# Exchanging heads in the loads of the last six pairs instead of in GpSimd's casts

## The chip, the cores and the metric

The kernel runs on one core of a Trainium2 chip. The metric is the device time of one execution in microseconds (us). The kernel before takes 314.71 us (median of 3 runs, 314.62 to 314.78). Profiles are of one execution each; their "span" goes from the first to the last instruction of the program, and the device time holds a little more around it.

The core has five engines that run side by side, each with its own queue of instructions in a fixed order: TensorE (PE; its weight loads are PEld), VectorE (DVE), ScalarE (ACT), GpSimd (POOL) and SyncE (SP), which in this kernel issues DMAs. They wait for each other through semaphores.

## The reference

A retention layer (attention with a decay in place of a softmax) and a bilinear feed-forward layer on its output.

```python
# q, k, v: [8 batches, 8 heads, 576 tokens, 64]
scores = scale * np.matmul(q, k.transpose(0, 1, 3, 2))
gamma = 1.0 - 2.0 ** (-5.0 - np.arange(H))
rel = pos[:, None] - pos[None, :]
Dmat = np.where(rel >= 0, gamma[:, None, None] ** rel, 0.0)
attn_out = np.matmul(scores * Dmat, v)
x = attn_out.transpose(0, 2, 1, 3).reshape(4608, 512)
a, b = x @ w_a, x @ w_b            # 512 -> 1536
out = (a * b) @ w_out              # 1536 -> 512
```

Inputs and the output are float32; the kernel multiplies in bfloat16.

## The kernel before

**Tiling.** The 4608 tokens are taken in 18 pairs of 256 tokens. For the first three the code works in steps of its own; from then on every pair n has two blocks of 128 tokens (kp = 0, 1), one token per partition, so that a pair's q, k or v is a tile of 128 partitions by 1024 float32: 2 blocks x 8 heads x 64. Pairs 15 and 17 (`LEFT`) gather the last 64 tokens of four batches each. The feed-forward layer works on blocks of 512 tokens (two pairs), with 12 slices of its hidden width. The last five blocks use combined sums of weights, rows and products (Strassen-like) to save matmuls.

**Why heads change places.** TensorE multiplies 64x64 pieces, four at a time, in the four quarters of its array. So the two heads of a head pair c and the two halves (64 tokens) of a block are matched crosswise: in partitions 64 to 127 of `qkb`, the bfloat16 tile that holds q and k of a pair, the two heads of each head pair stand in exchanged places (`keyed`, L662: `64 * (r ^ a)`). Before the change, GpSimd makes this exchange while it converts.

**A pair's way.** The function names and lines are those of the listing:
- `load_pair(n)` (L163): SyncE loads q, k and v from HBM into float32 tiles `qf`, `kf`, `vf` (L171), one DMA per block; for pairs 15 and 17 one per batch (four of 64 partitions). The tiles are in turn, two of each kind.
- `ahead(n)` (L564): GpSimd makes `qkb` and `vb`. For n >= `MIXED` (6) q is multiplied by a decay per token and head from the table `qs2` (`decayed_queries`: L579 for partitions 0 to 63, L584 for partitions 64 to 127, with the heads exchanged); k is converted (L605, and L609 with the exchange); v is multiplied by its decay from `vs2` (L616).
- `turn(n)` (L625): SyncE issues two DMA transposes, q and k of `qkb` into `qkT` (L633). For n > 10 it then calls `load_pair(n + 2)`.
- `stretch(n, n - 1)` (L847): TensorE opens the outputs of pair n - 1 from the states (L763), multiplies keys and values of pair n (`keyed`, L664), its scores (`matched`, L735, the first use of the pair's `qkT`) and closes the outputs of pair n - 1 (L776).

**Order.** The program is written out by hand: TensorE's matmuls are counted, and the list `todo` says at which count each of these functions is called. Each engine then runs its instructions in the order of these calls. On SyncE, load 12, the transposes of pair 11, load 13, the stores of a block's output (`store_mixed`, L997) and the transposes of pair 12 stand behind each other, and so on. On GpSimd the work of `ahead` shares the queue with sums of the output (L1071) and gated products (L1239). SyncE's DMAs count on eight semaphores in turn, so that a DMA also waits until the one eight places before it has landed.

**Tables.** `pair_tables` (L267) fills `vs2` and `qs2` in the opening phase: VectorE makes an index, and ScalarE takes exponentials of it, one for each head (L276, L278). `lgp` (L228) holds the logarithms of the decays, of even heads in partitions 0 to 63 and of odd heads in partitions 64 to 127.

Of the kernel before, what the change touches and what calls it, by code (L numbers as in the profile page):

```python
# [10 lines left out]
FP32 = mybir.dt.float32  # L11
BF16 = mybir.dt.bfloat16
INT32 = mybir.dt.int32
AF = mybir.ActivationFunctionType
# [4 lines left out]
def kernel(  # L19
# [10 lines left out]
    nc = tc.nc  # L30

    B, H, S, D = q.shape
    DM = H * D
# [4 lines left out]
    HP = H // 2  # L38
    scale = 1.0 / math.sqrt(D)
    gammas = [1.0 - 2.0 ** (-5.0 - h) for h in range(H)]  # L40
# [5 lines left out]
    LEFT = {NP - 3: 0, NP - 1: 1}  # L46
# [5 lines left out]
    PAIRS = [(0, 0), (1, 0), (2, 0), (0, 1), (1, 1), (2, 1)]  # L52
# [6 lines left out]
    def part_of(n):  # L59
        return PAIRS[n][1]  # L60
# [4 lines left out]
    def rows_of(n):  # L65

        if n not in LEFT:
            b, m = PAIRS[n]
            return [(kp, 0, 128, b, 256 * m + 128 * kp) for kp in (0, 1)]
        return [(i // 2, 64 * (i % 2), 64, 4 * LEFT[n] + i, S - 64)  # L70
                for i in range(4)]

    def pool(name, bufs, space=None):
        kw = {} if space is None else {"space": space}
        return ctx.enter_context(tc.tile_pool(name=name, bufs=bufs, **kw))

    const = pool("const", 1)
# [67 lines left out]
    def half(i):  # L145
        return slice(64 * i, 64 * i + 64)
# [10 lines left out]
    def staged(n, name, its_name):  # L157

        extra = n < MIXED + 3 and n % 3 == 2
        return (begin if extra else stage).tile(  # L160
            [128, 2 * DM], FP32, tag=name, name=its_name)

    def load_pair(n, which=(0, 1, 2)):  # L163
        if n >= NP:
            return
        paired.setdefault(n, {})
        for i in which:
            name, src = (("qf", q), ("kf", k), ("vf", v))[i]
            t = staged(n, name, name + "2")
            for kp, r0, m, b, s0 in rows_of(n):  # L170
                nc.sync.dma_start(  # L171
                    t[r0:r0 + m, kp * DM:(kp + 1) * DM]
                    .rearrange("p (h d) -> p h d", h=H),
                    src[b, :, s0:s0 + m, :].rearrange("h s d -> s h d"))
            paired[n][i] = t

    def load_step(n, hh, which, on=nc.sync):
# [11 lines left out]
    Q, K, V = 0, 1, 2  # L189
# [36 lines left out]
    idxp_f = const.tile([128, 2], FP32)  # L226
    nc.vector.tensor_copy(idxp_f, idxp_i)
    lgp = const.tile([128, HP], FP32)  # L228
    for c in range(HP):
        nc.vector.memset(lgp[0:64, c:c + 1], math.log(gammas[2 * c]))  # L230
        nc.vector.memset(lgp[64:128, c:c + 1], math.log(gammas[2 * c + 1]))
    biasq = const.tile([128, 1], FP32)
    nc.vector.memset(biasq, math.log(scale))
    vs = const.tile([128, H, 2], FP32)
    for h in range(H):
        nc.scalar.activation(vs[:, h, :], idxp_f, AF.Exp,
                             bias=0.0, scale=-math.log(gammas[h]))
# [10 lines left out]
    idxv = const.tile([128, 3, 2], FP32)  # L248
    vs2 = const.tile([128, 3, 2, H], FP32)

    qs2 = const.tile([128, 3, 2, H], FP32)
# [14 lines left out]

    def pair_tables(step):  # L267
        if step == 0:
            nc.vector.tensor_copy(idxv, idxv_i)
            nc.vector.tensor_scalar_add(idxv[:, 2, 1:2], idxv[:, 2, 1:2],  # L270
                                        -128.0)
            nc.vector.tensor_scalar_add(idxv[64:128, 2], idxv[64:128, 2],
                                        -64.0)
        else:
            for h in (2 * step - 2, 2 * step - 1):
                nc.scalar.activation(vs2[:, :, :, h], idxv, AF.Exp,  # L276
                                     bias=0.0, scale=-math.log(gammas[h]))
                nc.scalar.activation(qs2[:, :, :, h], idxv, AF.Exp,  # L278
                                     bias=biasq[:, 0:1],
                                     scale=math.log(gammas[h]))  # L280

    state_after = begin.tile([128, 2, HP, 128], BF16)
    own_sums = [begin.tile([128, HP, 64], FP32, name=f"own{n}")
# [280 lines left out]
    def ahead(n):  # L564


        qkb = nat.tile([128, 2, 2 * DM], BF16, tag="qkb", name="qkb2")
        vb = nat.tile([128, 2 * DM], BF16, tag="vb", name="vb2")
        halves = [slice(0, DM), slice(DM, 2 * DM)]
        whole = [slice(0, 2 * DM)]  # L570
        part = 2 if n in LEFT else part_of(n)

        def per_head(t):
            return t.rearrange("p (h d) -> p h d", d=D)

        def decayed_queries(t):
            by = qs2[:, part].rearrange("p k h -> p (k h)")
            for hs in (slice(0, H), slice(H, 2 * H)):
                nc.gpsimd.tensor_tensor(  # L579
                    per_head(qkb[0:64, Q])[:, hs], per_head(t[0:64])[:, hs],  # L580
                    by[0:64, hs].unsqueeze(2).to_broadcast([64, H, D]),
                    op=ALU.mult)
            for r in (0, 1):
                nc.gpsimd.tensor_tensor(  # L584
                    per_head(qkb[64:128, Q])[:, 1 - r::2],
                    per_head(t[64:128])[:, r::2],
                    by[64:128, r::2].unsqueeze(2).to_broadcast([64, H, D]),
                    op=ALU.mult)

        if n >= MIXED:  # L590
            decayed_queries(paired[n].pop(Q))
        if n >= BY_ACT:
            t = paired[n].pop(K)
            to, fro = (x.rearrange("p (j r d) -> p j r d", r=2, d=D)
                       for x in (qkb[64:128, K], t[64:128]))
            key_casts[n] = [
                lambda: nc.scalar.copy(qkb[0:64, K], t[0:64])] + [
                lambda r=r: nc.scalar.copy(to[:, :, 1 - r], fro[:, :, r])
                for r in (0, 1)]
            copies_due.extend([lambda: key_casts[n].pop(0)() if key_casts[n]  # L600
                               else None] * 3)
        for w in () if n >= BY_ACT else (K,) if n >= MIXED else (Q, K):
            t = paired[n].pop(w)
            for e in halves:
                nc.gpsimd.tensor_copy(qkb[0:64, w, e], t[0:64, e])  # L605
                to, fro = (x.rearrange("p (j r d) -> p j r d", r=2, d=D)
                           for x in (qkb[64:128, w, e], t[64:128, e]))
                for r in (0, 1):
                    nc.gpsimd.tensor_copy(to[:, :, 1 - r], fro[:, :, r])  # L609
        t = paired[n].pop(V)  # L610
        decay = (vs2[:, part].unsqueeze(3)
                 .to_broadcast([128, 2, H, D])
                 .rearrange("p k h d -> p (k h) d"))
        for e in halves:
            at = slice(e.start // D, e.stop // D)
            nc.gpsimd.tensor_tensor(  # L616
                vb[:, e].rearrange("p (h d) -> p h d", d=D),
                t[:, e].rearrange("p (h d) -> p h d", d=D),
                decay[:, at], op=ALU.mult)
        natural[FIRST + n, "pair"] = (qkb, vb)  # L620
# [4 lines left out]
    def turn(n):  # L625
        while key_casts.get(n):
            key_casts[n].pop(0)()
        qkb = of(natural, n)[0]
        qkT = qkt_pool.tile([128, 2, 2, HP, 128], BF16, tag="qkT",
                            name="qkT2")  # L630
        transposed[FIRST + n, "pair"] = qkT
        for w in (Q, K):
            nc.sync.dma_start_transpose(  # L633
                qkT[:, w].rearrange("p k c s -> p (k c) s"), qkb[:, w])
        if n > 10:
            load_pair(n + 2)
# [913 lines left out]
    for i, which in ((4, Q), (4, K), (4, V), (5, Q), (5, K), (5, V)):  # L1550
        load_step(*STEPS[i], which)
    load_pair(FIRST)
    load_pair(FIRST + 1, (Q,))


# [94 lines left out]
    for fn, places in ((ahead, casts), (turn, turns)):  # L1650
        todo += [(at, fn, (n,)) for n, at in places.items()]
# [46 lines left out]
```

## Time and profile before

| what | us |
|---|---|
| device time, median of 3 runs | 314.71 |
| device time of the profiled execution | 314.71 |
| its span | 313.0 |
| TensorE busy | 303.0 |
| GpSimd busy | 202.8 |
| VectorE busy | 224.0 |
| ScalarE busy | 156.0 |

The profile's page has the busy time of each engine, the chain of work that ended last (followed back from the last instruction), and groups of instructions by line and shape with their mean duration and the idle time of the engine before them. Its map of the span in 40 slices has these two rows, busy tenths of TensorE and of GpSimd:

```profile
PE   7899999999999999999999999999999999999994
...
POOL 3990079665996649867799769985999350035413
```

A slice is 7.8 us. TensorE is over 90% busy in all but the first two and the last. GpSimd is close to full in many slices between 40 and 245 us. The clock that TensorE was granted is 0.998 of full speed over the span.

### The profile page before, as it was taken

The page shows a single profiled execution, that of the slowest core. Times are in us where ns is not written, and L with a number is a line of the kernel's source. Part 1 is how long each engine was busy: PE and PEld are TensorE (multiplying, and loading weights), DVE is VectorE, ACT ScalarE, POOL GpSimd, SP SyncE. Part 2 cuts the span into 40 slices and gives each one's busy share as a digit, 9 for nine tenths or more (in the row PEclk, how much of TensorE's full clock was granted, in tenths as well). Part 3 has the DMA queues.
Part 4 walks back from the last instruction along what each step waited for, and adds up shares of the span by engine and source line. Part 5 has one row for each costly group of instructions (what it writes and reads, how often), then busy time and mean ns, then how long its engine had stood idle before and what let it go on. Part 6 is the DMA issues. An engine that isn't in the chain of part 4 may idle for free.

```text
span 313.0 us, 9645 instructions
## 1 busy us (share of the span) xinstructions
PE 303.0 (97%) x3922; PEld 198.6 (63%) x3955; DVE 224.0 (72%) x450; ACT 156.0 (50%) x351; POOL 202.8 (65%) x290
## 2 busy tenths in 40 slices
PE   7899999999999999999999999999999999999994
PEld 3554457868544554557874787468746875687774
DVE  5745337758757765768878886888679968877873
ACT  7755346626433554455455545544635554335530
POOL 3990079665996649867799769985999350035413
PEclk9999999999999999999999999999999999999999
DMA  8999999999999999999999989948703020013004
GB/s 213 256 202 207 247 240 198 197 216 182 208 171 231 174 204 191 218 244 285 190 260 228 179 180 227 192 83 182 213 10 70 24 112 2 2 53 85 1 2 134
DMA packets 144797, 50.97 MB, mean 163 GB/s; under 512 B 126576, under 2 KB 141680, under 8 KB 144752
## 3 DMA queue, kind: packets, MB, share of 16 engines
q1 hardware_dynamic: 138272, 45.10, 70.9%
q0 software_dynamic: 5808, 4.72, 9.6%
q8 instruction: 31, 0.51, 0.7%
q10 hardware_dynamic: 672, 0.52, 0.5%
q14 instruction: 14, 0.11, 0.1%
HBM read 37.75 MB, written 9.44 MB: 151 GB/s over the span
## 4 chain that ended last, share of the span: by engine, by line
PE 91%; DVE 2%; DMA 2%; SPq 2%; issue 2%; ACT 1%; DVEq 0%; ACTq 0%
PE m L1047 16%; PE pb L1419 13%; PE pa L1398 12%; PE pb L1284 9%; PE pa L1284 9%; PE po L1445 8%; PE lm L1227 7%; PE ls L1227 3%; DMA qf<-in_q_dram 2%; SPq L182 2%; PE la L1227 2%; PE po L933 2%; PE sc L735 2%; PE o L763 1%; PE kv L664 1%
## 5 line engine op out<-in xcount | busy, mean ns | idle before, releaser
L1424 DVE TENSOR_TENSOR hT<-ha,pb 128x512 bf16<-128x512 bf16 (+1 forms) x60 | 34.6, 579 | 32.4 <-PE pb L1419 28.4
L1419 PE MATMUL pb<-xT,wb_sb 128*128 128x512 bf16 (+1 forms) x237 | 49.9, 336 | 0.3
L1398 PE MATMUL pa<-xT,wa_sb 128*128 128x512 bf16 (+1 forms) x238 | 47.6, 326 | 0.5 <-issue 0.3
L1412 ACT CAST ha<-pa 128x512 bf16<-128x512 f32 (+1 forms) x60 | 29.8, 500 | 34.3 <-PE pa L1398 31.8
L1071 POOL TENSOR_TENSOR osb<-crossed,straight 128x256 f32<-128x256 f32 x24 | 17.5, 756 | 44.3 <-ACT crossed L1059 44.3
L1419 PEld LDWEIGHTS <-wb_sb 128*128 128x128 bf16 x240 | 23.4, 98 | 17.8 <-issue 0.5
L1398 PEld LDWEIGHTS <-wa_sb 128*128 128x128 bf16 x244 | 23.3, 98 | 16.5 <-DVE sums L691 0.2
L579 POOL TENSOR_TENSOR qkb<-qf,qs 64x512 bf16<-64x512 f32 x24 | 24.7, 1044 | 13.1 <-DMA qf<-in_q_dram 8.2
L1284 PE MATMUL pb<-xT,wb_sb 128*128 128x512 bf16 x125 | 32.1, 379 | 0.2
L616 POOL TENSOR_TENSOR vb<-vf,vs 128x512 bf16<-128x512 f32 x30 | 30.8, 1046 | 2.0 <-DMA vf<-in_v_dram 0.8
L1284 PE MATMUL pa<-xT,wa_sb 128*128 128x512 bf16 x119 | 31.4, 379 | 0.7 <-issue 0.3
L1047 PEld LDWEIGHTS <-hT 128*128 128x128 bf16 x288 | 28.1, 98 | 5.0 <-DVE hT L981 0.5
L1294 ACT CAST ha<-pa 128x512 bf16<-128x512 f32 x32 | 18.7, 585 | 24.6 <-PE pa L1284 24.6
L1297 DVE TENSOR_TENSOR hT<-ha,pb 128x512 bf16<-128x512 bf16 x32 | 21.9, 684 | 10.0 <-PE pb L1284 8.1
L609 POOL CAST qkb<-kf 64x256 bf16<-64x256 f32 x60 | 27.7, 488 | 1.5
L1445 PE MATMUL po<-wo_sb,hT 128*128 128x512 bf16 x113 | 26.7, 379 | 0.8 <-issue 0.6
L584 POOL TENSOR_TENSOR qkb<-qf,qs 64x512 bf16<-64x512 f32 x24 | 26.7, 1134 | 0.7
L1047 PE MATMUL m<-wo_sums,hsum 128*128 128x256 bf16 x216 | 25.7, 273 | 0.0
L981 DVE TENSOR_TENSOR hsum<-hT 128x512 bf16<-128x512 bf16 (+2 forms) x51 | 23.5, 493 | 0.5
L605 POOL CAST qkb<-kf 64x512 bf16<-64x512 f32 x30 | 20.3, 677 | 5.4 <-DMA kf<-in_k_dram 4.0
L1047 PEld LDWEIGHTS <-hsum 128*128 128x128 bf16 x216 | 21.1, 98 | 2.4
L1284 PEld LDWEIGHTS <-wb_sb 128*128 128x128 bf16 x128 | 12.3, 98 | 14.3
(159 smaller groups left out, 578.4 us busy)
## 6 DMA issues: line engine op xcount, KB each, us to landing
qf<-in_q_dram SPq DMA_DIRECT2D x32, 256.0 KB, 5.4
vf<-in_v_dram SPq DMA_DIRECT2D x32, 256.0 KB, 5.0
kf<-in_k_dram SPq DMA_DIRECT2D x31, 256.0 KB, 5.1
out_dram<-osb SPq DMA_DIRECT2D x9, 512.0 KB, 4.2
out_dram<-osb SPq DMA_DIRECT2D x22, 128.0 KB, 2.8
wo_sb<-in_moe_w_out_dram POOLq DMA_DIRECT2D x3, 512.0 KB, 15.9
out_dram<-osb SPq DMA_DIRECT2D x6, 256.0 KB, 4.1
qf<-in_q_dram SPq DMA_DIRECT2D x8, 128.0 KB, 3.3
```

The costliest lines, as they stand in the source:

```text
L579: nc.gpsimd.tensor_tensor(per_head(qkb[0:64, Q])[:, hs], per_head(t[0:64])[:, hs], by[0:64, hs].unsqueeze(2).to_broadcast([64, H, D]), op= ...
L584: nc.gpsimd.tensor_tensor(per_head(qkb[64:128, Q])[:, 1 - r::2], per_head(t[64:128])[:, r::2], by[64:128, r::2].unsqueeze(2).to_broadcast( ...
L609: nc.gpsimd.tensor_copy(to[:, :, 1 - r], fro[:, :, r])
L616: nc.gpsimd.tensor_tensor(vb[:, e].rearrange("p (h d) -> p h d", d=D), t[:, e].rearrange("p (h d) -> p h d", d=D), decay[:, at], op=ALU.mult)
L1047: nc.tensor.matmul(to, rows, cols, start=(begins and p == 0), stop=True, skip_group_check=True)
L1227: nc.tensor.matmul(to[:, m], w[:, c], x[:, c], start=(way in (1, 2, 5) and m == c == 0), stop=True, skip_group_check=True)
L1284: nc.tensor.matmul(p1, w[:, c, F * 128:F * 128 + 128], xT[:, c], start=(c == 0), stop=(c == NC - 1))
L1398: nc.tensor.matmul(pa[:, at:at + width], wa_sb[:, c, fs], xT[:, c, at:at + width], start=(c == at == 0), stop=(c == NC - 1), skip_group_ch ...
L1412: nc.scalar.copy(ha[:, 0:n], pa[:, 0:n])
L1419: nc.tensor.matmul(pb[:, 0:n], wb_sb[:, c, fs], xT[:, c], start=(c == 0), stop=(c == NC - 1))
L1424: nc.vector.tensor_tensor(hT[:, F, 0:n], has[F][:, 0:n], pb[:, 0:n], op=ALU.mult)
L1445: nc.tensor.matmul(po, hT[:, F, u * 128:(u + 1) * 128], wo_sb[:, F], start=(F == 0), stop=(F == NF - 1))
```

## The change

For pairs 12 to 17 (`PLACED = 12`) the loads of q and k already put the heads of tokens 64 to 127 of each block in exchanged places. A new function `places_of` gives, for each of the two blocks, three DMAs in place of one: partitions 0 to 63 with all eight heads, the even heads of partitions 64 to 127 into the odd places, and the odd heads into the even places. (For pairs 15 and 17 six take the place of four.) v is loaded as before. With the heads in place, GpSimd decays q with two products over 128 partitions in place of four over 64, and converts k with two casts over 128 partitions in place of two of 64x512 and four of 64x256.

The decay table `qs2` now holds, in partitions 64 to 127, the decay of the exchanged head; its exponentials take their factor from `lgp` or from a new table `lgq` (eight memsets on VectorE in `pair_tables`) in place of a constant. Pairs 6 to 11, which still exchange heads in GpSimd, read the table at `1 - r` instead of `r`.

```diff
+    PLACED = 12
+
+    def places_of(n, t, src):
+
+        heads = t.rearrange("p (k j r d) -> p k j r d", k=2, r=2, d=D)
+        if n in LEFT:
+            b0 = 4 * LEFT[n]
+            lower, upper = (src[b0 + a:b0 + 4:2, :, S - 64:S, :].rearrange(
+                "k (j r) s d -> s k j r d", r=2) for a in (0, 1))
+        else:
+            b, m = PAIRS[n]
+            lower, upper = (src[b, :, 256 * m:256 * m + 256, :].rearrange(
+                "(j r) (k a s) d -> a s k j r d", a=2, k=2, r=2)[a]
+                for a in (0, 1))
+        k = (0, 1)
+        return [(to[:, ks], fro[:, ks]) for ks in k for to, fro in (
+            (heads[0:64].rearrange("p k j r d -> p k (j r) d"),
+             lower.rearrange("s k j r d -> s k (j r) d")),
+            (heads[64:128, :, :, 1], upper[:, :, :, 0]),
+            (heads[64:128, :, :, 0], upper[:, :, :, 1]))]
...
-            for kp, r0, m, b, s0 in rows_of(n):
-                nc.sync.dma_start(
...
+            if i == V or n < PLACED:
+                for kp, r0, m, b, s0 in rows_of(n):
+                    nc.sync.dma_start(
...
+            else:
+                for to, fro in places_of(n, t, src):
+                    nc.sync.dma_start(to, fro)
...
+    lgq = const.tile([128, HP], FP32)
...
+            for c in range(HP):
+                for i in (0, 1):
+                    nc.vector.memset(lgq[half(i), c:c + 1],
+                                     math.log(gammas[2 * c + 1 - i]))
...
-                                     bias=biasq[:, 0:1],
-                                     scale=math.log(gammas[h]))
+                nc.scalar.activation(
+                    qs2[:, :, :, h], idxv, AF.Exp, bias=biasq[:, 0:1],
+                    scale=(lgq if h % 2 else lgp)[:, h // 2:h // 2 + 1])
...
+            own = slice(0, 128 if n >= PLACED else 64)
             for hs in (slice(0, H), slice(H, 2 * H)):
                 nc.gpsimd.tensor_tensor(
-                    per_head(qkb[0:64, Q])[:, hs], per_head(t[0:64])[:, hs],
-                    by[0:64, hs].unsqueeze(2).to_broadcast([64, H, D]),
+                    per_head(qkb[own, Q])[:, hs], per_head(t[own])[:, hs],
+                    by[own, hs].unsqueeze(2).to_broadcast([own.stop, H, D]),
                     op=ALU.mult)
-            for r in (0, 1):
+            for r in () if n >= PLACED else (0, 1):
                 nc.gpsimd.tensor_tensor(
                     per_head(qkb[64:128, Q])[:, 1 - r::2],
                     per_head(t[64:128])[:, r::2],
-                    by[64:128, r::2].unsqueeze(2).to_broadcast([64, H, D]),
+                    by[64:128, 1 - r::2].unsqueeze(2).to_broadcast([64, H, D]),
                     op=ALU.mult)
...
             for e in halves:
+                if n >= PLACED:
+                    nc.gpsimd.tensor_copy(qkb[:, w, e], t[:, e])
+                    continue
                 nc.gpsimd.tensor_copy(qkb[0:64, w, e], t[0:64, e])
```

More of the change, by code (lines that the diff above doesn't have):

```diff
@@ L169, in load_pair @@
             t = staged(n, name, name + "2")
-            for kp, r0, m, b, s0 in rows_of(n):
[L171 to L174, printed above, removed]
+            if i == V or n < PLACED:
+                for kp, r0, m, b, s0 in rows_of(n):
+                    nc.sync.dma_start(
+                        t[r0:r0 + m, kp * DM:(kp + 1) * DM]
+                        .rearrange("p (h d) -> p h d", h=H),
+                        src[b, :, s0:s0 + m, :].rearrange("h s d -> s h d"))
+            else:
+                for to, fro in places_of(n, t, src):
+                    nc.sync.dma_start(to, fro)
             paired[n][i] = t
@@ L277, in pair_tables @@
                                      bias=0.0, scale=-math.log(gammas[h]))
-                nc.scalar.activation(qs2[:, :, :, h], idxv, AF.Exp,
-                                     bias=biasq[:, 0:1],
-                                     scale=math.log(gammas[h]))
+                nc.scalar.activation(
+                    qs2[:, :, :, h], idxv, AF.Exp, bias=biasq[:, 0:1],
+                    scale=(lgq if h % 2 else lgp)[:, h // 2:h // 2 + 1])
     state_after = begin.tile([128, 2, HP, 128], BF16)
```

## The prediction

> **What bounds the kernel now.** I read the page first (busy shares, chain, costliest groups), then the rows of the stretch in which the changed code runs: SyncE's and TensorE's timeline, the landings there, and the waits of TensorE.
>
> ```profile
> span 313.0 us, 9645 instructions
> PE 303.0 (97%) x3922; PEld 198.6 (63%) x3955; DVE 224.0 (72%) x450; ACT 156.0 (50%) x351; POOL 202.8 (65%) x290
> ...
> PE 91%; DVE 2%; DMA 2%; SPq 2%; issue 2%; ACT 1%; DVEq 0%; ACTq 0%
> ```
>
> TensorE is busy for 303.0 of 313.0 us, and the chain that ended last is 91% TensorE; GpSimd (POOL) is not on it at all. Of TensorE's 10 idle us, 3.3 lie in the first 20 us and 4.1 after 298 us, there nearly all behind its last matmul. From 118 to 298 us the waits of TensorE hold three entries of 0.2 us or less, all put down to "issue", and with gaps of 0.05 us it is idle for some 1.2 us after 142.8, where the changed loads begin. So work taken from GpSimd returns time only where it ends one of these gaps, and none of them is released by GpSimd. What can happen is the reverse: something that TensorE needs arrives late. The rest of the prediction asks this.
>
> The costs on GpSimd:
>
> ```profile
> L579 POOL TENSOR_TENSOR qkb<-qf,qs 64x512 bf16<-64x512 f32 x24 | 24.7, 1044 | 13.1 <-DMA qf<-in_q_dram 8.2
> L616 POOL TENSOR_TENSOR vb<-vf,vs 128x512 bf16<-128x512 f32 x30 | 30.8, 1046 | 2.0 <-DMA vf<-in_v_dram 0.8
> L609 POOL CAST qkb<-kf 64x256 bf16<-64x256 f32 x60 | 27.7, 488 | 1.5
> L584 POOL TENSOR_TENSOR qkb<-qf,qs 64x512 bf16<-64x512 f32 x24 | 26.7, 1134 | 0.7
> L605 POOL CAST qkb<-kf 64x512 bf16<-64x512 f32 x30 | 20.3, 677 | 5.4 <-DMA kf<-in_k_dram 4.0
> ```
>
> 128 partitions cost the same as 64 (1046 against 1044 ns for 512 columns). And SyncE's queue (start, duration, waits included), where every load, store and DMA transpose stands in one order:
>
> ```profile
> 142.80 1.64 SPq L171 DMA_DIRECT2D qf<-in_q_dram  x2
> 144.48 3.57 SPq L171 DMA_DIRECT2D kf<-in_k_dram  x2
> 148.15 1.99 SPq L171 DMA_DIRECT2D vf<-in_v_dram  x2
> 150.25 4.15 SPq L633 DMA_TRANSPOSE qkT<-qkb  x2
> 154.45 1.25 SPq L171 DMA_DIRECT2D qf<-in_q_dram  x2
> 155.75 1.99 SPq L171 DMA_DIRECT2D kf<-in_k_dram  x2
> 157.83 2.44 SPq L171 DMA_DIRECT2D vf<-in_v_dram  x2
> 160.38 1.56 SPq L997 DMA_DIRECT2D out_dram<-osb  x2
> 162.04 5.45 SPq L633 DMA_TRANSPOSE qkT<-qkb  x2
> ...
> 178.61 2.78 SPq L171 DMA_DIRECT2D qf<-in_q_dram  x4
> ```
>
> These are: load 12, transposes of pair 11, load 13, the stores of a block, transposes of pair 12, and the q load of pair 15 (four of 64 partitions). SyncE has almost no free moment here. The last two views are the landing of the second transpose of pair 12 (issued at 164.39) and TensorE's first use of it:
>
> ```profile
> DMA to landing us min/median/max: 5.2/5.2/5.2
> ```
>
> ```profile
> 174.16 0.50 PE L735 MATMUL sc<-qkT 64*64 64x64 bf16 x32
> ```
>
> It lands at 169.5; the scores that need it start at 174.16: 4.6 us of cover.
>
> **The change, part by part.**
>
> *GpSimd.* Per changed pair, q goes from two L579 and two L584 (2 x 1.044 + 2 x 1.134 = 4.36 us) to two products of 128x512 (2 x 1.046 = 2.09): -2.3 us. k goes from two L605 and four L609 (2 x 0.677 + 4 x 0.488 = 3.31) to two casts of 128x512, whose like in the opening phase (L371) takes 0.61: 1.23, -2.1 us. That is -4.4 us a pair, -26 us over six pairs. On the path: 0, because no TensorE gap is GpSimd's; it only brings the transposes of pairs 14, 15 and 16 forward, which now wait for GpSimd (in the rows of pair 14, q is decayed from 185.69 to 189.84 and its first transpose starts at 189.86), and their cover is already 9 us or more.
>
> *Tables.* Eight memsets of 64x1 on VectorE at 24.3 us. Their like, L230, take 59 ns, spaced 0.1: 0.8 us. They push the index table, the eight exponentials behind it on ScalarE (24.88 to 26.14) and then its copy of 26.20 back by 0.8 us, and VectorE's gate product of 24.87 likewise. Four PSUM banks are in turn: the bank of the delayed product is free by 26.9 and is taken again at 27.9. Cost 0; if that cover were gone, at most 0.8 us. The exponentials' factor from a table instead of a constant stays one instruction of six elements (292 ns now); a doubling would be 0.3 us x 8 on an engine that is half idle.
>
> *SyncE.* This is the real price. q and k of pairs 12, 13, 14 and 16 go from 4 loads to 12, of 15 and 17 from 8 to 12: 40 more. The bytes and the 256-byte pieces stay. A load of 64 partitions by 8 heads (pair 15) takes 0.63 us and the next follows 0.68 after it; 64 by 4 heads is not in the trace. Bounds: the stores' shortest issue, 0.36 + 0.05 = 0.41, below, and the loads of 128x8x64 on a full queue, 0.9 to 1.1, above. I take 0.67, since the nearest row is pair 15's and 128x8x64 on a free queue takes 0.57 to 0.63 too: the issue hardly depends on size. Then q and k of a pair take 12 x 0.67 = 8.0 us and v 1.3: 9.3, against 7.4 (load 12, 142.80 to 150.19) and 5.9 (load 13). SyncE reaches the stores 1.9 + 3.4 = 5.3 us later, less up to 1.6 that pair 11's first transpose now spends on a full queue (2.79 against 1.25 us): 3.8 to 5.3 us late, at 164.2 to 165.7.
>
> *What is late next.* Behind the split loads stand the stores (nobody waits for these) and the two transposes of pair 12, which start at 165.2 to 166.8 instead of 162.04. They took 5.45 us on a full queue; with loads that SyncE hands over more slowly the queue is emptier, and 2.55 is enough. They then land by the later of two: 3.0 to 3.8 us after the second is issued (166.5 to 168.2), or 1.7 us after the second store (as now: 167.8 and 169.5), which itself lands 4.2 to 5.8 after issue. This gives 169.5 to 173.9, middle 171.8: 2.4 us before 174.16. On the path: 0, with a thin cover; each 0.1 us more per load costs 24 x 0.1 = 2.4 us of it. Pair 11's transposes (landed 156.4, used at 162.5) lose 1 to 2 us of 6. Pairs 13 to 17 have 8 to 15 us. A whole block (31.8 us) then holds 30 loads, 4 transposes and 2 stores on SyncE: 20.1 + 5.2 + 1.0 = 26 us, so the lateness does not build up. GpSimd's decays of pair 12 start at 153.8 behind the sums of L1071; k of load 12 lands by about 155 and is wanted at 155.9.
>
> **Sum.** 313.0 + 0 (GpSimd) + 0 (tables) + 0 (SyncE, under cover) = 313.0 us of span; the profiled execution took 314.71 with the 1.7 us around the span, which is the median of the runs. Forecast 314.7.
>
> **Rivals.**
>
> *Slower: the transposes of pair 12 miss the scores.* The place is the wait of TensorE at the scores of pair 12; it decides from a landing after 174.16, that is, when a split load costs over about 0.77 us on average (2.4/24 above 0.67), or the queue in front of the transposes does not empty. For it: SyncE's rows show hardly a pause, and issues of 1 us and more while the queue is full. Against it: pair 15's twelve loads of 64 partitions ran at 0.68 each without a break and landed in 3.3 to 3.6 us. At 0.80 the lateness grows by 3.1 us: landing 172.6 to 177, a stall of 0 to 2.9 us, middle 1.2: 315.9. At 1.0 it is 7.9 us, a stall of 5 to 6: about 320. TensorE never makes up a stall.
> The Trainium skill has a rule for this side: SBUF — State Buffer, section "Can I just issue two DMAs to hit both halves?", says that two transfers to the two partition halves serialize and that only one over all 128 partitions reaches all ports; its table gives 196 GB/s for half the partitions. By it the 2 MiB of q and k of two pairs would need an estimated 10.7 us, still under the 16 us of their issue, so the sum would stay. Pair 15's rows agree (128 KB every 0.68 us, 193 GB/s), but cannot tell the port from the issue, which sets the same pace there.
>
> *Faster: the freed GpSimd speeds its neighbours.* GpSimd's casts of one shape take 0.60 to 0.97 us, so something shares with it, and VectorE may run shorter with 26 us less beside it. Against it: no gap of TensorE after 142.8 is released by GpSimd, and VectorE releases one, 0.19 us at 303.6. All gaps there are 1.2 us: the most that could be won, 313.5; 314.0 for half.
> The Trainium skill's rule is in SBUF — State Buffer, section "Who interferes with whom": GpSimd and VectorE share a port pair as an exclusive lock. By it VectorE gains time; the trace agrees that casts beside it are slower, but here such time only lengthens VectorE's idle stretches before TensorE's results.
>
> *The load pattern does not shorten GpSimd's work* (the 128-partition products take twice as long): nothing changes on the path, 314.7; it belongs to the forecast.
>
> **How the numbers follow.** No change 0.70 (own range 314.4 to 315.0); late transposes 0.23; faster 0.07. I call 0.2%, 0.63 us, the least that can be told from no change. Late transposes lie mostly between 315.4 and 316.6 (0.14 of the 0.23), the rest above; so 314.2 to 316.6 holds a little over 8 in 10. Faster, same and slower are the three cases: 0.07, 0.70, 0.23.
>
> **What would show it.** Right: the split loads of pairs 12 to 14 stand 0.6 to 0.7 us apart; GpSimd's busy time falls by about 26 us to 177; the second transpose of pair 12 lands between 169.5 and 174; TensorE's waits after 142.8 stay under 1.5 us; the eight memsets delay no matmul. Wrong: an idle time of TensorE before the scores of pair 12, or before any later scores; issues of a split load near 1 us; GpSimd waiting for q or k so long that the sums and gated products queued behind it (L1071, L1239) hold up TensorE; or a TensorE gap that closes because GpSimd is free.

## The result, and the profile after

The changed kernel takes 318.22 us (median of 6 runs, 316.45 to 319.63); the kernel before, on the same chip, 314.81 us (6 runs, 314.62 to 315.23). The ratio is 1.0103, with a 95% interval of 1.0066 to 1.014: slower by 1%, where no change was forecast. The spread is part of the result. In all comparisons of this document, 89 executions of the kernel before lie between 314.42 and 315.84 us; the changed kernel was never seen below 315.77. One execution each of e2 (635.77 us) and of e15 (320.72 us) counts as slow and is left out of their ratios.

In the changed kernel, the lines of the steps have moved: the split loads are L199, the unsplit ones L193, the DMA transposes L667, the scores L769, GpSimd's products of q L610, its casts of k L637, its products of v L650.

The page of the profiled execution (319.12 us) first: busy times and the chain that ended last.

```profile
span 317.3 us, 9710 instructions
...
PE 307.9 (97%) x3955; PEld 199.8 (63%) x3955; DVE 223.0 (70%) x458; ACT 156.3 (49%) x351; POOL 175.4 (55%) x254
...
PE 86%; DMA 5%; SPq 2%; DVE 2%; ACT 1%; POOL 1%; issue 1%; DVEq 0%; ACTq 0%; POOLq 0%
```

GpSimd's busy time fell from 202.8 to 175.4 us, as intended, and the span still grew by 4.3. DMA has gone from 2% to 5% of the chain. (The count of TensorE's records, 3922 before and 3955 here, tells of records missing in the trace of before; the gaps there that were put down to "issue" are such holes.) GpSimd's groups, with different shapes kept apart:

```profile
L610 POOL TENSOR_TENSOR qkb<-qf,qs 128x512 bf16<-128x512 f32 x12 | 12.2, 1037 | 0.0
L637 POOL CAST qkb<-kf 128x512 bf16<-128x512 f32 x12 | 7.0, 606 | 1.1 <-DMA kf<-in_k_dram 1.1
```

So a product over 128 partitions takes 1.037 us and a cast 0.606 us. Now SyncE's timeline (start, duration, waits included; load 12, transposes of pair 11, load 13, stores, transposes of pair 12), of the same execution:

```profile
144.90 4.64 SPq L199 DMA_DIRECT2D qf<-in_q_dram  x6
149.58 4.76 SPq L199 DMA_DIRECT2D kf<-in_k_dram  x6
154.44 1.18 SPq L193 DMA_DIRECT2D vf<-in_v_dram  x2
155.73 3.31 SPq L667 DMA_TRANSPOSE qkT<-qkb  x2
159.09 3.96 SPq L199 DMA_DIRECT2D qf<-in_q_dram  x6
163.09 3.95 SPq L199 DMA_DIRECT2D kf<-in_k_dram  x6
167.14 1.73 SPq L193 DMA_DIRECT2D vf<-in_v_dram  x2
168.97 1.18 SPq L1031 DMA_DIRECT2D out_dram<-osb  x2
170.26 4.43 SPq L667 DMA_TRANSPOSE qkT<-qkb  x2
```

Six loads take 3.95 us where nothing holds them (0.66 each) and 4.6 to 4.8 where the queue is full. ("Full" is this text's word for stretches in which single issues take over 1 us; no view shows how full the queue is.) The transposes of pair 12 start at 170.26 instead of 162.04; 3.0 of these 8.2 us are a shift of the whole program (below). TensorE's waits from 118 to 310 us have an entry that the kernel before did not have:

```profile
PE sc L769 <- DMA qkT<-qkb: 0.5, 1, 0.5
```

It is the wait of the slower rival, at the scores of pair 12. But 0.5 us does not explain 4.3. The weight loads of the two kernels, matched one by one, give the shift at each place: 0.1 us at 14 us, 3.2 at 40, 3.0 at 160, 3.7 at 180 (behind the scores of pair 12) and 4.0 from 236 on. So most of this execution's loss came in the opening, long before the first split load. One execution of a kernel with such a spread is not enough; the profiles of five are compared below.

### The profile page after: what moved, and what is told of

It reads as the page before. It is cut to its first block, busy times and chain, and to the rows that moved or that the text cites. A ratio compares the mean times of both kernels' runs of the same rounds, so it can differ in the third digit from the quotient of the medians.

```text
span 317.3 us, 9710 instructions
## 1 busy us (share of the span) xinstructions
PE 307.9 (97%) x3955; PEld 199.8 (63%) x3955; DVE 223.0 (70%) x458; ACT 156.3 (49%) x351; POOL 175.4 (55%) x254
## 4 chain that ended last, share of the span: by engine, by line
PE 86%; DMA 5%; SPq 2%; DVE 2%; ACT 1%; POOL 1%; issue 1%; DVEq 0%; ACTq 0%; POOLq 0%
PE m L1081 16%; PE pb L1453 13%; PE pa L1432 12%; PE po L1479 8%; PE pa L1318 8%; PE pb L1318 7%; PE lm L1261 6%; DMA vf<-in_v_dram 3%; PE ls L1261 3%; SPq L207 2%; DMA qkT<-qkb 2%; PE la L1261 2%; PE po L967 2%; PE sc L769 2%; PE o L797 1%; PE o L810 1%
## 5 line engine op out<-in xcount | busy, mean ns | idle before, releaser
L1432 PE MATMUL pa<-xT,wa_sb 128*128 128x512 bf16 (+1 forms) x244 | 48.3, 327 | 0.0
L1446 ACT CAST ha<-pa 128x512 bf16<-128x512 f32 (+1 forms) x60 | 29.5, 499 | 34.5 <-PE pa L1432 28.6
L1432 PEld LDWEIGHTS <-wa_sb 128*128 128x128 bf16 x244 | 23.3, 98 | 16.5 <-DVE sums L725 0.2
L650 POOL TENSOR_TENSOR vb<-vf,vs 128x512 bf16<-128x512 f32 x30 | 31.6, 1072 | 2.5 <-DMA vf<-in_v_dram 1.7
L1318 PE MATMUL pa<-xT,wa_sb 128*128 128x512 bf16 x128 | 32.9, 379 | 0.0
L610 POOL TENSOR_TENSOR qkb<-qf,qs 64x512 bf16<-64x512 f32 (+1 forms) x24 | 25.0, 1055 | 13.6 <-DMA qf<-in_q_dram 5.2
L1479 PE MATMUL po<-wo_sb,hT 128*128 128x512 bf16 x120 | 27.8, 380 | 0.0
L1015 DVE TENSOR_TENSOR hsum<-hT 128x512 bf16<-128x512 bf16 (+2 forms) x51 | 21.2, 448 | 0.5
L1318 PEld LDWEIGHTS <-wa_sb 128*128 128x128 bf16 x128 | 12.1, 98 | 12.4
L778 DVE TENSOR_TENSOR sT<-sc,mask 128x512 bf16<-128x512 f32 x30 | 19.9, 683 | 0.0
L725 DVE TENSOR_TENSOR sums<-kv,sums 128x256 f32<-128x256 f32 x44 | 18.6, 423 | 1.6
```

The source lines that it names most:

```text
L610: nc.gpsimd.tensor_tensor(per_head(qkb[own, Q])[:, hs], per_head(t[own])[:, hs], by[own, hs].unsqueeze(2).to_broadcast([own.stop, H, D]), ...
L650: nc.gpsimd.tensor_tensor(vb[:, e].rearrange("p (h d) -> p h d", d=D), t[:, e].rearrange("p (h d) -> p h d", d=D), decay[:, at], op=ALU.mult)
L1015: lambda e=ways[i]: nc.vector.tensor_tensor(*e[:3], op=e[3]))
L1318: nc.tensor.matmul(p1, w[:, c, F * 128:F * 128 + 128], xT[:, c], start=(c == 0), stop=(c == NC - 1))
L1432: nc.tensor.matmul(pa[:, at:at + width], wa_sb[:, c, fs], xT[:, c, at:at + width], start=(c == at == 0), stop=(c == NC - 1), skip_group_ch ...
L1446: nc.scalar.copy(ha[:, 0:n], pa[:, 0:n])
```

## The experiments

**Theories.** A: the new tables shift every later tile in memory by 32 bytes, and that delays the opening. B: the code behind the opening delays it, by its new instructions or by the split loads. C: the opening is late by chance, in any kernel. D: SyncE is late, and the transposes of pair 12 with it. E: something in the changed program upsets the opening each time. F: the additional DMAs cost wherever they are issued. GpSimd's new work is a rival in itself.

### The tables and the shift: e1, e2, e3

e1_shift32 adds to the kernel before one unused tile, `pad = const.tile([128, HP], FP32)`, behind `lgp`. e2_after_aligned adds one to the changed kernel, so that the shift is 64 bytes. e3_tables_only is the changed kernel with `PLACED = NP`: its tables, but no split load and no 128-partition work.

> The kernel before with one unused 32-byte tile behind lgp: nothing computed changes, but every SBUF tile that is allocated behind it starts 32 bytes higher, as in the changed kernel (which has lgq there). Theory A (the opening is late because the tiles moved off a 64-byte boundary): the opening's last v load lands about 1.3 us later and the time rises by 0.8 to 4 us, to 315.5 to 319, with scatter between runs like the changed kernel's 316.45 to 319.63. Theory B (the code behind the opening, its instructions or the split loads, causes it): 314.7 to 315.2 as before. Theory C (the opening's lateness is scatter of the chip on that day, whatever the kernel): any kernel of this call shows it at times, the kernel before too.

> The changed kernel with a second 32-byte tile behind lgq, so that all tiles behind it are 64 bytes higher than before and on the same kind of boundary. Theory A: the opening is as before, and what is left is the stall of TensorE at the scores of pair 12 and some tenths after it: 0.5 to 1.0 us over before, 315.2 to 315.9. Theory B: 316.5 to 319.6 as the changed kernel.

> The changed kernel with PLACED = NP: tables, memsets and the 32-byte tile lgq are there, no load is split and GpSimd works as before. Theory A: 315.5 to 319, like the kernel before with the unused tile. Theory B with the split loads as the cause: 314.7 to 315.2. If the memsets or the exponentials cost something, this lies above the kernel with the unused tile by up to 0.8 us.

e1: 314.8 us, ratio 1.0 (0.999 to 1.0009). e2: 318.88 us (five executions, 316.07 to 319.91), ratio 1.0108 (1.0073 to 1.0143). e3: 314.78 us, ratio 1.0001 (0.9991 to 1.0011). Theory A fell, and of B the new instructions for the tables; C has no support, as none of the 29 executions of the kernel before in this comparison is above 315.84. The loss is in what `PLACED` switches on.

### The other four pairs: e4

```diff
-    PLACED = 12
+    PLACED = 14
```

(with the unused tile of e2.)

> The changed kernel with the second 32-byte tile and PLACED = 14: pairs 12 and 13, whose split loads stand ahead of the transposes of pair 12 on SyncE, are loaded and converted as before; pairs 14 to 17 keep the change. Theory (the stall at pair 12's scores is SyncE's lateness from these two loads, and boundaries cause the rest): no idle time of TensorE before any scores, time within 0.3 us of before, 314.6 to 315.1. If the boundary is not the cause, 316 or more.

315.26 us (314.73 to 316.44), ratio 1.0012 (1.0 to 1.0024). No wait at any scores, and 0.6 us of span lost in steps of 0.1 to 0.3 us in the stretches from 174 us on. Without pairs 12 and 13 nearly all of the loss is gone.

### The changed kernel again, four times: e5, e11, e13, e14

> The changed kernel once more, for a second profile: which of the pieces of the first one (opening late by 3.1 us with the clock halved for 3.4 us; 0.65 us at the scores of pair 12; 0.1 us at each later stretch) belong to the change and which to one execution. Theory D (SyncE's lateness): the opening is as before, and TensorE waits at the scores of pair 12 for the second transpose, for 1 to 4 us, as long as the time is over 315. Theory E (something in the changed program upsets the opening, and the clock with it): the opening is late again by 1 us or more.

> The changed kernel once more, for its profile alone: if it falls at 317.5 us or above, the profile shows what the higher executions lose beyond the wait at the scores of pair 12. Theory G: after a wait of over 1 us TensorE's clock is recorded at half for some 3.4 us, which costs 1.7 us, and the higher executions have one or two more such windows than the lower ones. Rival: the wait itself is longer in them (landing of the transposes later by 2 to 3 us), with the clock at 1.0.

> The changed kernel, for its profile. Theory D: the time is 314.7 us plus the wait at the scores of pair 12 (0 to 1.5 us) plus 0.7 to 1 us of gaps of 0.1 to 0.2 us behind it. Theory G: at 318 us or more there is besides a stretch of some 3.4 us at half clock (1.7 us), in front of which TensorE waited for over 1 us, at the scores of pair 12 or in the opening.

> As in the run before: one more profile of the changed kernel. Theory D: 314.7 us, plus the wait at the scores of pair 12 and up to 1 us of small gaps. Theory G: at 318 us or more also a stretch at half clock behind a wait of over 1 us.

With the first profile, ordered by time, all in us. "Pace" is the mean time per split load from the start of load 12 to its v, and the same for load 13 (for the first row 142.04 to 150.70 and 155.68 to 163.73: 16.71 / 24 = 0.70); the waits are TensorE's at the scores of pairs 12 and 16.

| execution | time | shift of the opening, at 40 us | pace | transposes of pair 12 start | wait, pair 12 | wait, pair 16 |
|---|---|---|---|---|---|---|
| e11 | 315.77 | 0.0 | 0.70 | 166.81 | 0.28 | none |
| e5 | 316.98 | 0.0 | 0.79 | 168.20 | 1.27 | none |
| e13 | 318.89 | 0.0 | 0.79 | 168.51 | 1.30 | 1.49 |
| first | 319.12 | 3.2 | 0.73 | 170.26 | 0.46 | none |
| e14 | 320.98 | 3.6 | 0.76 | 172.25 | 1.17 | 0.28 |

The wait at pair 12 is there in all five, and it grows with the pace of the split loads. At pair 16 it appears in two. The opening is late in two, so E does not hold in the form "each time". What is left (0.6 to 1.4 us of span in each) is in steps of 0.1 to 0.2 us at the stretches between; no view names what causes these. Here is SyncE's timeline in e13, from the transposes of pair 12 to those of pair 16:

```profile
168.51 5.30 SPq L667 DMA_TRANSPOSE qkT<-qkb  x2
173.87 3.96 SPq L199 DMA_DIRECT2D qf<-in_q_dram  x6
177.88 4.62 SPq L199 DMA_DIRECT2D kf<-in_k_dram  x6
182.60 1.18 SPq L193 DMA_DIRECT2D vf<-in_v_dram  x2
183.88 3.30 SPq L667 DMA_TRANSPOSE qkT<-qkb  x2
187.22 4.81 SPq L199 DMA_DIRECT2D qf<-in_q_dram  x6
192.08 3.94 SPq L199 DMA_DIRECT2D kf<-in_k_dram  x6
196.12 3.54 SPq L193 DMA_DIRECT2D vf<-in_v_dram  x4
199.77 1.03 SPq L1031 DMA_DIRECT2D out_dram<-osb  x2
200.91 4.44 SPq L667 DMA_TRANSPOSE qkT<-qkb  x2
...
233.49 8.04 SPq L667 DMA_TRANSPOSE qkT<-qkb  x4
```

Each line begins where the line above it ends: SyncE has no pause at all, and GpSimd's work on q and k of each of these pairs was done before SyncE reached its transposes. A block of two pairs takes 200.91 - 168.51 = 32.4 us here, and the next one, to 233.49, 32.6; TensorE's block takes 31.9 (scores of pairs 12 and 14 at 174.16 and 206.07 before). So the lateness grows in both blocks, until it shows at pair 16. In the other four executions the first of these blocks takes 32.1 to 32.5 us as well, but the second 30.7 to 31.2: there SyncE catches up a little. In TensorE's timeline of e13, both waits (in brackets, with what ended them):

```profile
176.00 0.45 PE L769 MATMUL sc<-qkT 64*64 64x64 bf16 x32 [1.30 <-DMA qkT<-qkb]
...
241.52 0.45 PE L769 MATMUL sc<-qkT 64*64 64x64 bf16 x32 [1.49 <-DMA qkT<-qkb]
```

Theory G of the expectations (a wait of over 1 us halves the clock for some 3.4 us) does not hold as it was put. The two slowest of the five have such a stretch, but in the opening; e13, at 318.89 us, has none, and behind its waits of 1.30 and 1.49 us the windows show 1.00.

### One part of the change alone: e7, e8

e7_split_only makes as many loads, but to the heads' own places, with GpSimd working as before. e8_pool_only has GpSimd's 128-partition work on unsplit loads (so the heads of pairs 12 to 17 are not exchanged there).

```diff
 e7
-            (heads[64:128, :, :, 1], upper[:, :, :, 0]),
-            (heads[64:128, :, :, 0], upper[:, :, :, 1]))]
+            (heads[64:128, :, :, 0], upper[:, :, :, 0]),
+            (heads[64:128, :, :, 1], upper[:, :, :, 1]))]
 ...
 e8
-            if i == V or n < PLACED:
+            if True:
```

> The split loads alone: the same 12 DMAs for q and k of pairs 12 to 17, but each piece goes to its own place, and GpSimd exchanges heads as before. Theory D: as the changed kernel or slower, 316 to 320, with TensorE idle before the scores of pair 12, since SyncE is as late and GpSimd gives nothing. If GpSimd's new work were part of the loss (by its contention with VectorE), 314.7 to 315.2.

> GpSimd's part alone: two products and two casts over 128 partitions for pairs 12 to 17, with the loads of before (the heads are then not exchanged, so the output differs from the reference). Theory D: 314.5 to 315.0: 26 us less work on GpSimd and no change in time, as none of TensorE's waits is GpSimd's. Theory E with GpSimd's code as the cause: 316 or more.

e7: 317.56 us (315.75 to 319.08), ratio 1.0079 (1.0049 to 1.011). e8: 314.83 us (314.61 to 315.52), ratio 1.0 (0.9991 to 1.0008). The two add up: the split loads alone lose what the change loses, within the intervals, and 28 us less work on GpSimd (174.5 us in e8) are worth nothing. e7's profile was of a short execution (315.86) without a wait at the scores.

### Another order on SyncE: e6

e6_late13 issues load 13 behind the transposes of pair 12:

```diff
-        if n > 10:
+        if n == 12:
+            load_pair(13)
+        if n > 11:
             load_pair(n + 2)
```

> The changed kernel, but SyncE issues load 13 behind the transposes of pair 12 instead of ahead of them (same DMAs, same work on every engine). Theory D: the transposes of pair 12 are issued some 8 us earlier and land long before 174 us; no idle time at their scores; 314.8 to 315.4 and little scatter. Theory E: 316 to 320 as before, since nothing in the opening differs.

316.88 us (316.3 to 318.1), ratio 1.0064 (1.0046 to 1.0082). The wait at pair 12 is gone; but loads 13 and 14 now stand in a row, and SyncE gets to the transposes of pair 14 at 202.12. TensorE waits there for 1.44 us, and the time stays above the 314.8 to 315.4 us that theory D gave. The wait goes where two loads stand ahead of transposes: this order only moves it.

### Fewer extra loads: e10, e16

e10_only12 treats pair 12 alone in the new way (`PLACED = (12,)`, with `n in PLACED`); e16_q_only treats q of all six pairs so, and loads and casts k as before.

> The changed kernel with only pair 12 loaded in split form and decayed on 128 partitions; pairs 13 to 17 as in the kernel before. Theory D: the transposes of pair 12 are late by about the share of load 12 in the delay, 3 us of the 5 to 8, and land by about 174.9 or earlier: 0 to 0.7 us lost, 314.8 to 315.6 us. Theory F (loss grows with the number of extra DMAs, 8 of 40 here): 315.1 to 315.6 us with the gaps behind 160 us gone. Equal times; the rows of SyncE and the gaps tell them apart.

> The changed kernel with the exchange in the loads of q alone: k is loaded and cast as in the kernel before, so SyncE has 20 extra loads instead of 40. Theory D: a block of two pairs on SyncE falls by 12 loads less 6 of the old form, some 4 us, to 28 to 29 us, under TensorE's 31.9, so lateness doesn't build up and pair 16 never waits; the transposes of pair 12 start some 3 us earlier than in the changed kernel, at 164 to 167 us, and land before 174.2: 314.7 to 315.3 us, and GpSimd is still relieved by some 14 us. Rival (every split load costs): half of the loss of the changed kernel, 316 to 317.5 us.

e10: 314.91 us (314.55 to 317.01), ratio 1.0013 (0.9995 to 1.0031). The profile, of an execution of 314.61, has the transposes of pair 12 at 164.40 and no wait; two of the ten executions (316.07 and 317.01) lie above all of the kernel before. e16: 315.25 us (314.98 to 315.83), ratio 1.0008 (0.9997 to 1.0018), with GpSimd at 186.4 us. In e16 the transposes of pairs 12, 14 and 16 stand so on SyncE:

```profile
165.07 5.12 SPq L664 DMA_TRANSPOSE qkT<-qkb  x2
...
194.55 5.15 SPq L664 DMA_TRANSPOSE qkT<-qkb  x2
...
224.16 10.58 SPq L664 DMA_TRANSPOSE qkT<-qkb  x4
```

That is 29.5 and 29.6 us per block. The loss does not fall by half with half of the extra loads, as it would if each cost something; within the interval it is gone. That fits a queue that has come below its full load.

### As many loads of another form: e15

e15_by_heads is the kernel before, with the q and k loads of the six pairs cut by heads into as many as in the changed kernel: pieces of 128 partitions by two or three heads, for pairs 15 and 17 of 64 partitions by four or eight.

```diff
+                cuts = (0, H)
+                if i != V and n > 11:
+                    cuts = ((0, 3, 6, H) if len(rows) == 2 else
+                            (0, 4, H) if x % 2 else (0, H))
+                for h0, h1 in zip(cuts, cuts[1:]):
```

> The kernel before, with GpSimd's work and all places as they were; only the q and k loads of pairs 12 to 17 are cut by heads into as many loads as in the changed kernel (six per tensor, 40 more in all), of 128 partitions by two or three heads where the pair has two loads per tensor, and of 64 partitions by four or eight heads for pairs 15 and 17. Theory D (the number of loads on SyncE): each load takes 0.57 to 0.65 us, SyncE works without a pause, the transposes of pair 12 start at 167 to 169 us, and the time is 315.7 us or more, as with the split loads with GpSimd unchanged (317.56). Rival (the form: 64 partitions at a time): the loads of two heads are shorter, 0.4 to 0.5 us, SyncE is not late, 314.7 to 315.2 us.

316.46 us (seven executions, 314.74 to 318.72; the kernel before 315.04 there), ratio 1.0077 (1.0039 to 1.0115). Each side was right in part. With 128 partitions at a time in four of the six pairs the loss is still there, so the form of 64 partitions in all six is not needed; but those loads are cheaper, 0.47 to 0.50 us on a free queue, some 0.54 apart, as the rival had it. The profile is of the fastest execution, 314.74 us, with the transposes of pair 12, from 166.66 on, in time, and 31.7 us from there to those of pair 14: just under TensorE's block. That the slower executions lost at the scores is inferred.

### The extra loads on other engines: e9, e12

```diff
-                for to, fro in places_of(n, t, src):
-                    nc.sync.dma_start(to, fro)
+                for x, (to, fro) in enumerate(places_of(n, t, src)):
+                    (nc.scalar if x % 3 else nc.sync).dma_start(to, fro)
```

e12 has `nc.gpsimd` in the place of `nc.scalar`.

> The changed kernel, but the eight loads per pair that fill partitions 64 to 127 of q and k are issued by ScalarE; SyncE keeps the four that fill partitions 0 to 63, and v, so it has no more loads than in the kernel before. Theory D (the loss is SyncE's queue being late at the transposes): no wait of TensorE at the scores of pair 12, transposes of pair 12 issued before 166 us, and 314.7 to 315.3 us, unless ScalarE is held up by its issues (48 in all, at 0.1 us or more each, ScalarE is half idle) or by a load that waits for its staging buffer, which would show as TensorE gaps released by ScalarE. Theory F (the loss is made by the smaller and more numerous DMAs wherever they are issued, by the traffic or by the length of the program): still 316 to 319.5 us with the same scatter, small gaps in the 64x64 matmuls from 143 us on.

> The changed kernel, but the eight loads per pair that fill partitions 64 to 127 of q and k are issued by GpSimd; SyncE keeps four loads for q and k and two for v, as in the kernel before. Theory D (SyncE's order): SyncE reaches the transposes of pair 12 by 163 to 165 us if the data are there, no wait at their scores, and 314.7 to 315.3 us. If GpSimd's issues are dear (1 us each would be 48 us, 8 a pair, more than the 4.4 us a pair that it gains) its casts come late and TensorE waits behind DMA transposes that SyncE issues late for want of casts: 315.5 us or more, with SyncE standing idle in front of its transposes. Theory F (number of DMAs): 316 to 319.5 us, SyncE not late, no idle time in front of its transposes.

e9: 354.04 us, ratio 1.1239 (1.1218 to 1.126). The waits of ScalarE and of TensorE in e9 (the second number is how often, the third the longest):

```profile
ACT xT L868 <- DMA kf<-in_k_dram: 34.6, 3, 20.9
```

```profile
PE pa L1432 <- ACT ha L1446: 17.8, 1, 17.8
```

ScalarE stood at its loads for up to 20.9 us, with the conversions that TensorE needs queued behind them. Of these, 12.4 us passed before the first load was issued, at 141.48. Its buffer had been free since 127.8, when GpSimd ended the decays of pair 10; the view puts the wait down to a load of k, and one landed just then (GpSimd's cast of it starts at 141.44). The issues of the eight loads took the other 8.5 us. So e9 says nothing of the disputed loads.

e12: 321.75 us, ratio 1.0239 (1.0192 to 1.0286). SyncE issues the transposes of pair 12 at 164.17, and there is no wait at any of pairs 12 to 17, which is what D says; theory F, which gave 316 to 319.5 us for such a case, has no support here. The loss came from the other side, as TensorE's waits show:

```profile
PE m L1081 <- DVE hT L1331: 2.6, 2, 1.5
PE pb L1318 <- DVE hT L1331: 1.8, 1, 1.8
```

Those products of VectorE were late because a sum ahead of them took long. The timelines of VectorE, and of GpSimd, in e12:

```profile
173.50 0.69 DVE L1331 TENSOR_TENSOR hT<-ha,pb 128x512 bf16<-128x512 bf16 x1 [0.23 <-ACT ha L1328]
174.11 3.73 DVE L1015 TENSOR_TENSOR hsum<-hT 128x1024 bf16<-128x1024 bf16 x1
177.75 0.68 DVE L1331 TENSOR_TENSOR hT<-ha,pb 128x512 bf16<-128x512 bf16 x1
```

```profile
169.16 2.47 POOL L199 DMA_DIRECT2D qf<-in_q_dram  x4
171.62 2.46 POOL L199 DMA_DIRECT2D kf<-in_k_dram  x4
174.07 2.07 POOL L610 TENSOR_TENSOR qkb<-qf,qs 128x512 bf16<-128x512 f32 x2
176.05 1.18 POOL L637 CAST qkb<-kf 128x512 bf16<-128x512 f32 x2
```

GpSimd needs 0.62 us per issue, 4.9 a pair, more than the 4.4 that it was spared, and its products come later, in an unbroken row, over VectorE's sums. That they are what lengthened the sum of 3.73 us is read from the overlap in time.

## Why the prediction was wrong

**What held.** GpSimd: 27.4 us less, 4.6 a pair where 4.4 were forecast, worth 0 (e8). The tables: 0 (e3); the exponentials start 0.7 us late and delay no matmul. The split load's own price: 0.61 to 0.63 us, 0.66 to 0.68 apart, where the queue is free. That TensorE is bound by its own work also held: no experiment was faster than the kernel before. VectorE's sums did get shorter beside a freed GpSimd, as the faster rival had it (figures below), and TensorE gained nothing by it.

**The first step that failed: "with loads that SyncE hands over more slowly the queue is emptier, and 2.55 is enough".** The queue was not emptier. The transposes of pair 12 took 4.4 to 5.3 us in the five executions, where 2.55 were forecast and 5.45 were measured before, and they started at 166.8 to 168.6 (the opening's shift taken off), not at 165.2 to 166.8, since some split loads take 1 to 2 us while the queue is full: the mean pace is 0.70 to 0.79, not 0.67. In e13 the second transpose landed at 175.96, 4.9 us after its issue, where 3.0 to 3.8 had been taken. The landing forecast for 171.8 came behind 174.16, that shift taken off, in all five. The rival's condition was met: the queue did not empty in any of the five, and in two the mean pace was over 0.77. The stall that it gave for 0.80, 0 to 2.9 us with 1.2 as the middle, holds the 1.27 and 1.30 that e5 and e13 show at 0.79. That its middle fits is in part luck: its own landings (171.8 + 3.1 = 174.9) lie only 0.7 us behind 174.16. Its time of 315.9 was too low, since it had neither the later wait nor the small steps: e5 took 316.98. Its chance, 0.23, was too low: the rows of before had issues of over 1 us on a full queue, and the forecast took the free queue's price for all of them.

**The second: "20.1 + 5.2 + 1.0 = 26 us, so the lateness does not build up".** The first block takes 32.1 to 32.5 us in the five, the second 30.7 to 32.6. In e13 the first takes 32.4 us, against TensorE's 31.9: transposes 8.7 (5.2 forecast), 24 split loads 17.6 (16.1), six v loads 4.9 (4.0), stores 1.1 (1.0). So a queue thought to be idle for 5 us a block had 1.2 us to spare at most, little absorbed a slow issue, and pair 16, given "8 to 15 us" of cover, waited in two executions of five. e16, with 29.5 us, has enough to spare.

**What was not foreseen: the opening.** It costs 3 us and more in two of five executions, outside every rival, and puts these above the range; e5 and e13 lie above it by the waits and the small steps alone. In the first profile the last v load of the opening is issued at 8.66 us as usual, but lands at 15.53. Of the sixteen completions that the trace records for it, fifteen are in by 13.90; only one is late. In e14 fourteen are in by 13.79 and the last two come at 14.39 and 15.93, while in the 16 other profiles all sixteen are in by 14.04. The load's consumers on ScalarE are late, and TensorE idles for 1.14 and 0.39 us; then its clock is at half for a while. Why loads of the opening are late in a kernel whose split loads come 130 us later is open. That it goes with the extra loads is shown only by counting. Of 89 executions of the kernel before none exceeds 315.84 us. And a stretch at half clock lowers the mean granted clock that is listed for every execution: it is 0.995 or less in ten executions of kernels with extra loads on SyncE or GpSimd (one of them e10, with 8 extra loads), and 0.997 or more in the 83 listed of the kernel before and in the 34 of e1, e3 and e8, which have none.

**What stays open**: this, and the steps of 0.1 to 0.2 us at the later stretches.

## What to carry to other kernels

Count the issuing queue like an engine: its busy time per block, with transposes and loads at the price of the full queue, against the block time of the engine that sets the pace. Work spared on an engine that no wait names is worth nothing; work added to a queue cost nothing here that the medians show with 8 or 20 extra loads, and with 40 it cost time, with a spread from run to run that is itself a sign. A load placed on a computing engine's queue blocks all that stands behind it there, so it belongs there only when everything it waits for, its buffer and earlier loads alike, is surely done.

## What the runs showed of the hardware

**Issue time hardly follows size.** A split load of 64 partitions by 4 heads (64 KB) takes 0.61 us on SyncE, as one of 64 by 8 heads does, and two or three heads of 128 partitions (64 or 96 KB) take 0.47 to 0.50. The Trainium skill, page "DMA: Bandwidth & Descriptors", section "Issuing engines are not separate DMA queues", says that issuing from several engines saves only the sequencer's time to start a transfer, which it calls usually small relative to the transfer. The trace agrees for one load, not for a queue of them: 0.61 us is small beside the 2.3 to 4.4 us to landing (e13), but 24 of them, with the other loads, the stores and the transposes, fill a block. And issued from ScalarE or GpSimd, the loads cost more than they had on SyncE: 354.04 and 321.75 us against 318.22.

**VectorE beside a busy GpSimd.** A bfloat16 sum of 128x1024 on VectorE, 0.69 us in most cases of the changed kernel, took 3.73 us in e12 while GpSimd ran products and casts without a pause; the longest such sum of the kernel before between 118 and 245 us took 1.36. On average the twelve `hsum` sums of this shape take 943 ns in the kernel before, 913 in e7, where GpSimd works as before, 748 in the changed kernel and 703 in e8: VectorE pays for GpSimd's work there.

**The clock after the opening's waits.** Windows of the first profile of the changed kernel (length, TensorE's busy time and matmuls, granted clock, DMA share, GB/s):

```profile
14.00:16.00 2.00, 0.80 (x37) 1.00 1.42 194
16.00:18.00 2.00, 1.51 (x53) 1.00 1.26 167
18.00:20.00 2.00, 2.00 (x13) 0.53 1.00 128
20.00:22.00 2.00, 2.00 (x10) 0.62 1.27 190
22.00:24.00 2.00, 2.00 (x11) 1.00 1.30 200
```

After 4 us in which TensorE was busy for 2.31, its clock is at half from about 18.0 to 21.4 us, which costs some 1.7 us, half of that stretch. The Trainium skill, page "TensorE: Matmul & The Clock Gate", section "What's actually happening", has the array at half clock after an idle window of about 3.4 us, and back at full after a busy one. The length of the slow stretch agrees; the idle time ahead of it was shorter, 1.5 us in the two waits. In the 3.41 us just before the half-clock stretch TensorE was busy for 1.78 us (1.86 in e14, likewise in the opening); in e13 it was busy for 1.99 of the 3.41 us from 240.10, and after its waits at 176 and 241 us the clock stayed at 1.00.

One execution of e2 took 635.77 us, with TensorE busy for 628 of a span of 634 us and the same matmuls at 589 ns instead of 336. Its clock is listed as 1.0, but its page, alone of all, has no row of the granted clock and its trace no record of one, so that figure says nothing. That the array ran at half clock throughout fits the durations and isn't shown; no cause is seen.
